# A conformer branch backward on one core: hand-made order of heads and weights, wide loads, and the place of small zero-column DMAs

## Chip, cores, metric

One core of one Trainium2 chip. The metric is the device time of one execution in microseconds, the median of the runs of a kernel. PE is the tensor engine, DVE the vector, ACT the scalar, POOL the GpSimd engine, SP the engine that issues most DMAs.

## The reference

Forward and vector-Jacobian product of one block with an attention branch and a local branch, B, T, D, K = 2, 4000, 144, 5, all bf16; the kernel returns the output and the gradients of all eight inputs.

```python
def _fwd_reference(x, w_qkv, w_att_out, w_mlp_in, dw_csgu, w_mlp_out, dw_merge, w_merge):
    xa = _layernorm(x, axis=-1)
    qkv = jnp.einsum('btd,de->bte', xa, w_qkv)
    ...
    p = _softmax(scores, axis=-1)
    attn = jnp.einsum('bts,bsd->btd', p, v)
    glob = jnp.einsum('btd,de->bte', attn, w_att_out)
    h = _gelu(jnp.einsum('btd,de->bte', xc, w_mlp_in))
    ...                       # u, g; layernorm of g; five taps of dw_csgu give gc
    loc = jnp.einsum('btd,de->bte', u * gc, w_mlp_out)
    m = jnp.concatenate([glob, loc], axis=-1)
    ...                       # five taps of dw_merge
    m = m + mc
    return x + jnp.einsum('btc,cd->btd', m, w_merge)

def reference(..., grad_out):
    _out, _vjp = jax.vjp(_f, x, w_qkv, ...)
    return (_out, *_vjp(grad_out))
```

## The kernel before

Each of the two batches runs a head (layer norm, transposes, projections of x and of the gradient, group by group), an attention, and a tail (sums and output). Batch 0's head makes the fused weights as well. The parts that matter here follow; "..." marks cuts.

The taps of the fused weights, one small product for each column of taps:

```python
            for kt in range(2):
                for kk in range(5):
                    if h == 0:
                        nc.vector.tensor_scalar(A[:, kt, 4 - kk, :], UT[h][:, kt, :], W.wm[:, h, kt, kk:kk + 1], None, op0=ALU.mult)
                    else:
                        nc.gpsimd.tensor_scalar(A[:, kt, 4 - kk, :], UT[h][:, kt, :], W.wm[:, h, kt, kk:kk + 1], 1.0, op0=ALU.mult, op1=ALU.mult)
                    nc.gpsimd.tensor_scalar(Bz[:, kt, 4 - kk, :], Wmh[:, h, kt, 128:D], W.wm[:, h, kt, kk:kk + 1], 1.0, op0=ALU.mult, op1=ALU.mult)
```

The head's loop, whose engine order a scheduler settles. The second half of the weights comes after it:

```python
        for s in range(NGR + 2):
            if s < NGR:
                stA(s)                     # gradient: transposes, goT, go80
            if 0 <= s - 1 < NGR:
                stT(s - 1)                 # normalised x: transposes, xaT and R
            if s == NGR:
                nc.sync.dma_start(S.R_d[:], R[112:128, :])
                ...                        # loads of slices of R into ra, rb: four in batch 0, eight in batch 1
            if 0 <= s - 2 < NGR:
                stB(s - 2, ...)            # pq, pb, Q_t, dug, B_t
            ...
        if wts:
            wts.second(ps_t, ps_2)
```

Memory for shifted rows. Its edges must be zero, so its construction sends two tiny DMAs. The local branch makes two of these a batch and then asks for its first rows of R, stored by the head; the tail makes two more:

```python
class Taps:
    def __init__(self, k, name):
        self.a = k.tc.dram_tile([80, self.L], BF, name=name)
        ...
            self.nc.sync.dma_start(self.a[:, 2:4], k.zero[0:80, 0:2])
            self.nc.sync.dma_start(self.a[:, self.L - 4:self.L - 2], k.zero[0:80, 0:2])

def local_steps(k, W, b, S, es, ps, Q):
    ...
    gnC = Chan(k, W, wk, ps, "gnC%d" % b)      # each holds one Taps
    dgC = Chan(k, W, wk, ps, "dgC%d" % b)
    ...
    def load_R(p):
        nc.sync.dma_start(Rz[p % 2][112:128, :], S.R_d[:, p * 256:(p + 1) * 256])
    load_R(0)
```

The tail of batch 0 ends with a store of sums. Its buffer `grs` lies in a pool that is given up with the tail; the next head's pools take over that memory:

```python
            grs = pp.tile([128, 4, D], F32, name="grs")
            for n_ in range(2):
                nc.scalar.copy(grs[:, 2 * n_:2 * n_ + 2, :], ...)
            nc.sync.dma_start(k.A.gr_d[:], grs[:])
        ...
        # phase_head of the next batch
        first = S.ab.tile([128, 16, 128], BF, tag="ST", bufs=3, name="go80f")
```

## Time and profile before

| quantity | value |
|---|---|
| time | 1294.5 us, median of 3 (1293.1 to 1294.8) |
| span of the profiled execution | 1288.0 us (that execution took 1289.9) |
| PE busy | 1211.8 us, 94% |
| granted clock | 0.993 |

The profiled execution was 3 to 5 us faster than the timed ones.

How to read what follows. A stage is a window in us from the start of the span. A wait line has who waited (engine, output tile, source line), "<-", who ended the wait, then total us, number of waits and the longest. A chain line has start, duration and what ran. A timeline line has start, duration, engine, line, operation and tiles; "SPq" is SP's issue of a DMA, and the DMA itself goes on after it. Names that come back often: gs are gradient rows as loaded, g is POOL's copy of their narrow part, and go80f holds that part transposed; pq and pb are the head's products of a group; pS and pD are the score products of attention, and X the products that follow from them; ph is the local branch's first product, which reads Rz, the rows of R loaded back; EF are the tail's sums for weight gradients; hT is ACT's copy of the tail's transposes pt, and po are its output products. The prediction shows the stage table, the waits and the chain of this kernel.

### The profile page before, as it was taken

What the parts mean: (1) busy time and instruction counts of PE and PEld (TensorE: products, weight loads), DVE (VectorE), ACT (ScalarE), POOL (GpSimd) and SP (SyncE); (2) the same over time, 40 slices, a digit from 0 to 9 for tenths busy, and PEclk for the clock granted to TensorE, in tenths of its full rate; (3) what the DMA queues carried; (4) which work ended last, traced back from release to release, by engine and by line L of the source; (5) the groups of instructions that cost most, each with busy time, mean ns of one, the idle gap of its engine ahead of it and who ended that gap; (6) DMA issues with size and microseconds to landing.
All of it is one profiled execution on the core that took longest, in us unless ns stands there. A gap on an engine that the chain in (4) does not pass through costs nothing.

```text
span 1288.0 us, 39900 instructions
## 1 busy us (share of the span) xinstructions
PE 1211.8 (94%) x15116; PEld 949.9 (74%) x15116; DVE 962.3 (75%) x3293; ACT 843.5 (65%) x2498; POOL 558.8 (43%) x1033
## 2 busy tenths in 40 slices
PE   4899999999999999998989999999999999998996
PEld 2657777777777777788975777777777777778994
DVE  4656778888888788857735677888878878885674
ACT  2667777767767766546646767777777767664542
POOL 6412444545444453257611244444544445324650
PEclk9999999999999999999999999999999999999998
DMA  6378989898989989887775889899888999987861
GB/s 185 88 142 147 156 155 159 155 167 151 161 151 159 170 155 165 151 190 216 202 220 109 152 156 152 153 169 170 148 160 153 154 170 155 164 154 182 238 168 29
DMA packets 634223, 205.51 MB, mean 160 GB/s; under 512 B 577183, under 2 KB 631556, under 8 KB 633988
## 3 DMA queue, kind: packets, MB, share of 16 engines
q1 hardware_dynamic: 627472, 197.54, 80.6%
q10 hardware_dynamic: 6548, 5.33, 1.7%
q8 instruction: 120, 1.97, 0.6%
q14 instruction: 83, 0.68, 0.2%
HBM read 46.22 MB, written 21.79 MB: 53 GB/s over the span
## 4 chain that ended last, share of the span: by engine, by line
PE 71%; DVE 13%; DMA 4%; issue 4%; ACT 4%; POOL 3%; SPq 1%; ACTq 0%; DVEq 0%; POOLq 0%
PE y L1911 15%; PE pS L1865 9%; PE X L1933 9%; PE X L1934 8%; PE pD L1865 7%; PE pS L1861 5%; DVE Sm L1875 5%; PE pc L1573 3%; PE pb L1467 2%; PE po L2088 2%; PE EF L2063 1%; DVE jg L1792 1%; PE gr L2159 1%; DVE acc L1949 1%; ACT Qs L1894 1%
## 5 line engine op out<-in xcount | busy, mean ns | idle before, releaser
L1875 DVE SCALAR_TENSOR_TENSOR Sm<-pD,Pm 128x500 bf16<-128x500 f32 x512 | 325.7, 673 | 80.3 <-PE pD L1865 47.6
L1873 ACT ACTIVATE Pm<-pS 128x500 bf16<-128x500 f32 x512 | 295.5, 586 | 41.2 <-PE pS L1865 38.3
L1933 PE MATMUL X<-Qs,Sm 128*128 128x144 bf16 x2048 | 285.6, 226 | 9.3 <-DVE acc L1949 8.9
L1946 POOL TENSOR_TENSOR acc<-xs,acc 128x432 f32<-128x432 f32 x150 | 168.5, 1123 | 280.5 <-ACT xs L1945 280.0
L1934 PE MATMUL X<-Bt,Pm 128*128 128x144 bf16 x2048 | 285.4, 226 | 0.7 <-DVE Bt L1898 0.7
L1934 PEld LDWEIGHTS <-Pm 128*128 128x128 bf16 x2048 | 199.9, 98 | 11.9 <-issue 11.3
L1933 PEld LDWEIGHTS <-Sm 128*128 128x128 bf16 x2048 | 199.8, 98 | 1.5 <-issue 0.9
L1911 PEld LDWEIGHTS <-PT 128*128 128x128 bf16 x2048 | 136.5, 97 | 30.7 <-issue 2.4
L1911 PEld LDWEIGHTS <-ST 128*128 128x128 bf16 x2048 | 136.4, 97 | 27.6
L1945 ACT COPY xs<-X 128x432 f32<-128x432 f32 x150 | 77.9, 519 | 111.4 <-PE X L1934 103.4
L1949 DVE TENSOR_TENSOR acc<-X,acc 128x432 f32<-128x432 f32 x180 | 104.0, 578 | 53.9 <-PE X L1934 53.2
L1873 ACT ACTIVATION_READ_ACCUMULATOR Pm<-pS 128x1 f32 x512 | 105.0, 205 | 0.0
L1861 PE MATMUL pD<-rb,QBr 16*128 16x500 bf16 x448 | 96.0, 378 | 3.3 <-DVE Sm L1875 2.8
L1865 PEld LDWEIGHTS <-BTm 128*128 128x128 bf16 x512 | 49.8, 98 | 59.9 <-issue 1.6
L1861 PE MATMUL pS<-rb,QBr 16*128 16x500 bf16 x448 | 91.9, 380 | 0.1
L1792 DVE SCALAR_TENSOR_TENSOR jg<-gnC,dgC 128x256 bf16<-128x256 bf16 x160 | 89.6, 560 | 1.0
L1921 POOL TENSOR_TENSOR B_t<-zd,yd 128x144 bf16<-128x144 f32 x64 | 34.0, 531 | 113.0 <-ACT zd L1920 112.7
L1865 PEld LDWEIGHTS <-QTm 128*128 128x128 bf16 x512 | 29.1, 97 | 72.5 <-issue 72.5
L1865 PE MATMUL pS<-rb,QTm 128*128 128x500 bf16 x256 | 76.9, 382 | 0.0
L1865 PE MATMUL pS<-ra,QTm 128*128 128x500 bf16 x256 | 76.5, 381 | 0.0
L1911 PE MATMUL y<-rb,PT 128*128 128x144 bf16 x1024 | 74.3, 226 | 1.0 <-ACT zd L1920 1.0
L1911 PE MATMUL y<-ra,PT 128*128 128x144 bf16 x1024 | 74.3, 226 | 1.1 <-ACT zd L1920 1.1
(626 smaller groups left out, 2895.0 us busy)
## 6 DMA issues: line engine op xcount, KB each, us to landing
gs<-in_grad_out_dram SPq DMA_DIRECT2D x24, 720.0 KB
dh_d<-dh SPq DMA_DIRECT2D x32, 144.0 KB
dhr<-dh_d SPq DMA_DIRECT2D x16, 288.0 KB
gs<-in_grad_out_dram SPq DMA_DIRECT2D x8, 540.0 KB
xg<-in_x_dram SPq DMA_DIRECT2D x21, 144.0 KB
dug_d<-dug SPq DMA_DIRECT2D x16, 144.0 KB
dug<-dug_d SPq DMA_DIRECT2D x32, 72.0 KB
ug_d<-ug SPq DMA_DIRECT2D x32, 72.0 KB
```

The source lines that it names most:

```text
L1573: nc.tensor.matmul(pc[:, q, 0:128], t[:, q * 128 + m:q * 128 + m + 128], W.dg[:, (4 - m) if back else m, :], start=(m == 0), stop=(m == 4))
L1792: nc.vector.scalar_tensor_tensor(jg[:], a_[:, m:m + 256], 1.0, d_[:, 2:258], op0=ALU.mult, op1=ALU.mult, accum_out=dws[:, p, m:m + 1])
L1861: nc.tensor.matmul(o_[h][:, 0:SC], jt[i // 4][2][rr, i % 4, :], S.XR[c2][rr, 0:SC], start=True, stop=False)
L1865: nc.tensor.matmul(o_[h][:, 0:SC], jt[i // 4][w][:, i % 4, :], S.xaT[:, c0:c0 + SC], start=False, stop=True)
L1873: nc.scalar.activation(P[:, pb, c1:c1 + SC], o_[h][:, 0:SC], ACT.Exp, accum_out=ld8[:, 0, n_:n_ + 1])
L1875: nc.vector.scalar_tensor_tensor(Sm[:, pb, c1:c1 + SC], o_[h][:, 0:SC], 1.0, P[:, pb, c1:c1 + SC], op0=ALU.mult, op1=ALU.mult, accum_out=l ...
L1911: nc.tensor.matmul(y[:, w, :], src[:, jj, :], S.xaa[:, j, :], start=(j == 0), stop=(j == NBK - 1))
L1933: nc.tensor.matmul(X[:, jj, :], Sm[:, i % NP, j * 128:(j + 1) * 128], Qs[:, i % 4, :], start=(kk == 0 and jj == 0), stop=False, skip_group ...
L1934: nc.tensor.matmul(X[:, jj, :], P[:, i % NP, j * 128:(j + 1) * 128], Bt[:, i % 4, :], start=False, stop=(kk == 1), skip_group_check=True)
L1945: nc.scalar.copy(xs[:, 0:nj, :], X[:, 0:nj, :])
L1946: nc.gpsimd.tensor_tensor(a_, xs[:, 0:nj, :], a_, op=ALU.add)
L1949: nc.vector.tensor_tensor(a_, X[:, 0:nj, :], a_, op=ALU.add)
```

## The change

The intent: less idle PE outside attention. Parts: (1) tap products as wide broadcast operations; (2) loads in order of need, with masks, pads and zeros made while they travel; (3) the head in a hand-made order instead of the scheduler's, with the second half of the weights as pieces between groups; (4) in tail 0, the gradient loads of the next batch a step earlier, its normalise a step later, the reload (`fill`) half a step later; (5) zero columns of all four Taps of a batch sent as its attention begins.

```diff
-        for s in range(NGR + 2):
-            ...
-        if wts:
-            wts.second(ps_t, ps_2)
+        with tc.manual_schedule():
+            ...                                  # heads, taps1, keys, taps, rows, groups 0 and 1
+            for n in range(-1, NGR):
+                if 1 <= n + 2 < NGR:
+                    stT(n + 2)
+                if n == 3:
+                    jit0()
+                if n >= 0:
+                    stB(n, *tiles())
+                if 1 <= n + 2 < NGR:
+                    stA(n + 2)
+                if wts and n + 3 < NGR:
+                    nrm.shift(n + 3)
+                    nrm.apply(n + 3)
+                ...                              # narrow, stats, power, take_go, dug stores
+                if n == 5:
+                    spread()                     # R_d store and the slices of R
+                if n == 4:
+                    jit()
+                if rest:
+                    next(rest, None)             # a piece of the second half of the weights
@@ taps
+            nc.vector.tensor_tensor(self.A[0][:, kt], self.UT[0][:, kt, :].unsqueeze(1).to_broadcast([128, 5, D]),
+                                    self.wr[:, 0, kt, :].unsqueeze(2).to_broadcast([128, 5, D]), op=ALU.mult)
+            ...                                  # Bz on DVE the same way, A[1] on POOL
@@ local_steps
+    zero = on.tile([128, 2], BF, name="lo_zero")
+    nc.gpsimd.memset(zero[:], 0.0)
-    gnC = Chan(k, W, wk, ps, "gnC%d" % b)
-    dgC = Chan(k, W, wk, ps, "dgC%d" % b)
+    gnC = Chan(k, W, wk, ps, "gnC%d" % b, zero)
+    dgC = Chan(k, W, wk, ps, "dgC%d" % b, zero)
+    S.taps = [Taps(k, n + "80_%d" % b, zero) for n in ("y", "u")]
     ...
     load_R(0)
@@ attention
-        local_steps(k, W, b, S, es, ps_f, Q)
         with tc.manual_schedule():
+            local_steps(k, W, b, S, es, ps_f, Q)
@@ tail
+                if hf == 0 and 0 <= g - 2 < NGR:
+                    fill(g - 2)
                 ...
-                if hf == 1 and 0 <= g - 1 < NGR:
-                    fill(g - 1)
-                    for lag, f_ in ((4, nrm.apply), (3, nrm.power), (2, nrm.stats), (1, nrm.load)):
+                    for lag, f_ in ((5, nrm.apply), (4, nrm.shift), (3, nrm.power), (2, nrm.stats), (1, nrm.load)):
-                    if NPR <= h < NPR + 3:
-                        take_go(k, nxt, 1, h - NPR, nrm.ld)
+                    if NPR + 2 <= h < NPR + 4:
+                        narrow_go(k, nxt, h - NPR - 2, nrm.ld)
+                if nrm and NPR - 1 <= h < NPR + 2:
+                    take_go(k, nxt, 1, h - NPR + 1, nrm.ld)
```

(Cut: the weights' own code, two PSUM pools with 4 and 3 buffers instead of 3 and 4, the wide x loads, one normalise in four from DVE to POOL.)

## The prediction

> **What bounds the kernel now.** I began with the busy time by stage, since the 94% mean of PE (TensorE) says nothing about where the rest is. Each row gives the window, its length, the busy time (and instructions) of PE, PE's weight loads, DVE (VectorE), ACT (ScalarE) and POOL (GpSimd), then granted clock, DMA share and GB/s.
>
> ```profile
> 0.00:64.00 64.00, 40.98 (x359) 28.89 (x359) 34.98 (x208) 30.42 (x84) 32.76 (x95) 0.99 0.49 136
> 64.00:557.00 493.00, 480.70 (x5808) 362.10 (x5808) 391.22 (x1275) 346.30 (x1049) 207.79 (x355) 0.99 0.89 157
> 557.00:650.00 93.00, 86.74 (x1374) 84.42 (x1372) 61.49 (x243) 54.79 (x143) 56.87 (x114) 1.00 0.76 210
> 650.00:680.00 30.00, 25.66 (x290) 22.06 (x287) 12.31 (x36) 16.68 (x44) 5.58 (x16) 0.94 0.66 195
> 680.00:1173.00 493.00, 480.61 (x5850) 363.42 (x5848) 392.51 (x1276) 346.14 (x1047) 207.99 (x355) 1.00 0.90 156
> 1173.00:1288.00 115.00, 97.11 (x1450) 89.04 (x1447) 69.80 (x255) 49.11 (x134) 47.79 (x100) 0.97 0.54 151
> ```
>
> The rows are head, attention, tail of batch 0, then the same of batch 1. The two attentions take 986 of 1288 us and PE is busy for 97.5% of them; the change hardly touches them, so they stay. What it can win is idle PE in the rest: 23 us in head 0, 6.3 in tail 0, 4.3 in head 1, 17.9 in the last tail (12 of them after 1245 us, in the end sums that are not changed). Some 40 us at most.
>
> Second, PE's waits in head 0 (total us, times, longest), and the chain of waits through it (start, length, what).
>
> ```profile
> PE pr L1431 <- POOL g L1428: 8.4, 3, 7.0
> PE pm L1425 <- DMA gs<-in_grad_out_dram: 5.7, 1, 5.7
> ```
>
> ```profile
> 4.26 4.98 DMA gs<-in_grad_out_dram
> ...
> 9.83 1.04 POOL rstdx L1376
> ...
> 18.06 2.41 POOL w_Bz L1224 x8
> 20.47 0.35 POOL w_A L1223
> ...
> 26.83 0.25 POOL w_Bz L1224
> 27.08 0.44 POOL g L1428
> 27.57 0.65 PE pr L1431 x4
> ...
> 63.80 0.53 PE pS L1861
> ```
>
> From 18 to 27 us POOL makes 30 tap products (20 w_Bz of a mean 293 ns, 10 w_A of 381 ns in the table of groups: 9.7 us), and the g copy that PE needs stands behind them: PE waits 7.0 us in one piece, though every input of the copy has long landed. The loop over eight groups then runs from 28 to 58 us.
>
> Third, windows where the clock or PE looked odd in the 40 slices (28 to 58 is the loop, 58 to 66 the weight work behind it, 62 to 69 the first steps of attention, 652 to 660 the start of head 1).
>
> ```profile
> 28.00:58.00 30.00, 24.75 (x249) 19.36 (x247) 20.00 (x101) 19.93 (x53) 14.01 (x31) 1.00 0.34 95
> 58.00:66.00 8.00, 7.96 (x59) 4.68 (x59) 3.61 (x24) 4.93 (x21) 0.62 (x2) 0.77 0.51 136
> 62.00:69.00 7.00, 7.00 (x37) 4.11 (x37) 1.17 (x10) 4.16 (x16) 0.62 (x2) 0.52 0.33 87
> 652.00:656.00 4.00, 0.40 (x4) 0.34 (x5) 0.11 (x1) 0.85 (x2) 2.09 (x8) 1.00 1.06 308
> 656.00:660.00 4.00, 3.64 (x35) 3.50 (x35) 1.60 (x5) 1.57 (x3) 0.46 (x1) 0.57 0.80 270
> ```
>
> In the loop all engines have room: PE 82%, DVE and ACT 67%. The weight work is 7.6 us for which no group work is left to share PE, and around it the clock drops to about half, so 62 to 69 us is PE "busy" at half the work. Head 1 shows the same pair: 3.6 us of idle PE, then 3.5 us at 0.57.
>
> Fourth, what head 1's idle waits for, in its chain, and the issue times of the SP queue and PE at the start of attention 0.
>
> ```profile
> 650.48 5.29 DMA gr_d<-grs
> 655.89 0.43 DVE go80f L1434
> ```
>
> ```profile
> 67.39 0.83 SPq L1669 DMA_DIRECT2D Rz<-R_d  x2
> 68.28 0.41 SPq L1515 DMA_DIRECT2D y<-w_zero  x1
> ```
>
> The first Rz matmul of attention starts at 69.72: 2.3 us from issue to use, with five zero-column DMAs ahead of it on that queue and three behind.
>
> **What the Trainium skill says.** "TensorE: Matmul & The Clock Gate", Part 1, HAM clock gate: an idle array runs at 1.2 GHz and gets 2.4 GHz after about 3.4 us of sustained work. The trace agrees: 0.57 for about 3.5 us after a 3.6 us gap. "GPSIMD Engine Reference", 3.1 Elementwise: a tensor_tensor costs some 2.6 cycles an element on GpSimd against 1 on the DVE. Here POOL's 128x432 product takes 1123 ns, 2.6 ns an element, so dearer than the page's 2.2; small ones are nearly all fixed cost (128x16 in 293 ns, 128x144 in 381). "Perfetto Trace Analysis", TensorE instruction: ACT, DVE and GpSimd are strict FIFO, as g behind the taps shows. "DMA: Bandwidth & Descriptors", Two DMAs through the same engine are not ordered: a load of stored data must wait for the store's completion. R_d to Rz and y to r are such pairs, so in a hand-made order the place of each store and load on its queue sets when data arrives.
>
> **The change, part by part.**
>
> Taps in head 0. 40 small products become a few wide ones with a broadcast tap: A of the first half and Bz to DVE (2 of 128x720, some 0.8 us each, estimated at one element a cycle, and a small one), A of the second half to POOL in two of 720 elements, 720 x 2.6 = 1.87 us each. 9.7 us of POOL become 3.7, in two pieces between groups. The 7.0 us stall goes.
>
> Start. Loads are issued in order of need and masks, pads and zeros are made meanwhile. Group 0's x is one DMA and issued first: landed near 2.8 us, its statistics done at 5.2, the rstd power (1.04 us a time on POOL) at 7.5, one wide tap product until 9.4, g of group 0 at 10.8, its transposes at 12.5, the weight rows at 15.4 us. There the loop starts, against 28.
>
> Loop. PE has about 3.2 us a group including a share of the weight work, so it doesn't bound. With a hand-made order each group passes around one cycle of in-order ACT: transposes stT .46, pq .25, pb 2 x .73, latency .17, dug .34, B_t .32, goT copy .6, the ACT applies .92, semaphores .05 = 4.6 us, from the durations of these groups in the trace of before. Before, the scheduler ran 3.57 us a group. So: end of pb(0) at 22.3, four cycles to 40.7, then three lighter groups and the queued weight pieces, 9.9 us: the loop ends near 50.6 us (57.8 before), and nothing of the 7.6 us weight tail follows, since it lies in the loop's gaps. Attention could begin near 51 in place of 65.3.
>
> New wait on Rz. In the new order all eight zero-column DMAs of a batch stand on SP after the last dug store and ahead of the Rz load: 8 x .43 = 3.5 us, and 2.3 to landing with issue, plus .4 for the store: Rz lands at loop end + 6.2. PE gets there at + 2.7 to 3.3 (pS and history matmuls first). So PE waits about 3 us in both batches. First Rz matmul: 50.6 + 6.2 = 56.8, against 69.7: gain 12.8 us.
>
> Head 1. The grad loads are issued a step earlier and the narrow copies of two groups move to the tail, so the 5.3 us gr_d store no longer holds up the transposes: 3.6 us of idle and 1.7 of cold clock go, 4 to 5 us in all, of which the Rz wait of 3 us takes most, and nine more DMAs on SP about 0.6. Net 0.7.
>
> Tails. The y and u reloads (fill) move from the middle of a step to the start of the next, and ACT, which issues them, no longer stands before its hT copies; in the last tail PE waits 2.7 us for hT in two waits, in tail 0 about 1.3. The g wait of tail 0 (4.2 us in 3) should shrink with the earlier loads and a later apply. I count 3 us for both tails.
>
> Sum: 12.8 + 0.7 + 3.0 = 16.5 us. 1294.5 - 16.5 = 1278.
>
> **Rivals.** (a) All of it hides: the Rz wait doesn't come because the queue drains before the loop ends (the stores of early groups are long out), the loop holds 3.3 to 3.8 us a group, and head 0 ends at 46. Then head 0 gains 19, head 1 5, tails 4: 28 us, 1266. For it: 67% busy DVE and ACT; against it: the cycle adds up to 4.6 from measured parts. (b) New waits take the gain: PE waits on R copies now on ACT, on Rz and on the late reload in the tails, where a reload moved half a step (about 2.7 us) later has only its former slack of 5.57 us DMA against the step to live on. Then head 0 gains 9, head 1 loses 2, tails 0 or -2: 1287 to 1290. For it: two stores and loads in a row per group, whose order is now fixed. (c) The clock: a loop with PE 65 to 80% busy could be granted half speed, some 3 us more; against it, the loop of before at 82% held 1.00. The cold stretch could also just move to the Rz wait, as a gap of 3 us is close to the 3.4 of the page; 1 to 2 us a batch.
>
> **Range and chances.** Head 0 is 12.8 +- 5, the other two +- 3 each: 7 in all. Range 1268 to 1288, prediction 1278. The 2% line is 1268.6, a gain of 25.9 us, out of 40 us idle: it needs (a) nearly whole, 0.13. Slower by 2% needs a loss of 26 us where only heads and tails were touched: 0.01. Within 2%: 0.86.
>
> **What would show each step.** Start: first pb matmul at 16 to 18 us, no POOL wait of PE over 2 us. Loop: pb of successive groups 4 to 5 us apart for groups 1 to 4, waits of PE on ACT. End: first pS near 51 us, no run of weight matmuls alone. Rz: a PE wait of about 3 us on the DMA of Rz, in each batch, behind eight zero-column issues on SP. Head 1: no 3.6 us gap at its start, clock 1.00 there. Tails: waits on hT under 1 us. The prediction is wrong if attention begins before 47 or after 56 us, if PE doesn't wait for Rz, or if the attention windows of 493 us change by more than 2 us, which I take as untouched.

## The result

The changed kernel took 1289.5 us (median of 4, 1288.4 to 1293.5), the kernel before 1293.9 (median of 4). The ratio is 0.997, with a 95% interval of 0.995 to 1.000. A ratio is the mean time of one kernel's fast runs over that of the other's of the same rounds, so it is not quite the ratio of the medians. The profiled span is 1286.6 us against 1288.0.

Some 16 us were forecast and about 4 came. The stage table of the changed kernel, with bounds moved to where its stages lie, shows PE as idle as before; the columns are those of the prediction's stage table.

```profile
0.00:51.00 51.00, 38.51 (x369) 28.38 (x370) 34.44 (x174) 30.19 (x83) 32.05 (x74) 1.00 0.67 187
51.00:547.00 496.00, 479.79 (x5804) 361.50 (x5803) 391.21 (x1273) 346.23 (x1045) 208.54 (x354) 1.00 0.90 154
547.00:640.00 93.00, 87.21 (x1373) 84.50 (x1371) 61.53 (x243) 54.25 (x144) 56.60 (x113) 1.00 0.76 206
640.00:670.00 30.00, 25.43 (x285) 21.79 (x283) 12.27 (x37) 16.21 (x42) 5.16 (x16) 0.89 0.63 187
670.00:1171.00 501.00, 482.83 (x5853) 364.10 (x5852) 391.57 (x1276) 347.18 (x1048) 209.48 (x356) 0.99 0.90 154
```

Row 1: the head needs 51 us up to attention where it needed 64, and PE idles 12.5 us in it instead of 23. Row 5: the second attention stage now takes 501 us for the PE work of 493.

Windows cut by hand blur a loss at a border. I therefore took, in both traces, the start of the same matmuls as marks: the first and last X product of each attention and the last EF product of each tail. Lengths of the stages between the marks, in us:

| stage | before | after | change |
|---|---|---|---|
| start to first X (head 0 and first steps of attention) | 96.90 | 85.91 | -10.99 |
| attention 0 | 465.78 | 466.33 | +0.55 |
| tail 0 | 69.87 | 70.04 | +0.17 |
| last EF to first X of batch 1 (head 1) | 77.41 | 85.76 | +8.35 |
| attention 1 | 465.73 | 465.47 | -0.26 |
| tail 1 | 69.34 | 68.20 | -1.14 |
| end sums and close | 42.97 | 44.85 | +1.88 |
| sum | 1288.01 | 1286.56 | -1.45 |

Head 0 won 11 us and head 1 gave back 8.4. PE's waits in the changed kernel, first around head 0, then around head 1:

```profile
PE ph L1804 <- DMA Rz<-R_d: 3.1, 1, 3.1
PE fw L1360 <- DVE w_c L1361: 3.0, 1, 3.0
PE tp L1478 <- POOL g L1436: 1.8, 1, 1.8
```

```profile
PE ph L1804 <- DMA Rz<-R_d: 5.8, 1, 5.8
PE tp L1473 <- DVE go80f L1481: 4.2, 1, 4.2
```

POOL's 7.0 us are gone, and there is no weight tail behind the loop: the last pb ends at 50.85 us and the first pS starts at 50.78. Two waits on Rz have come, and the wait on go80f is still there. The chain shows both in head 1, and SP's issues show why Rz is late.

```profile
641.39 5.18 DMA gr_d<-grs
646.69 0.43 DVE go80f L1481
...
677.46 1.89 DMA Rz<-R_d
679.48 0.40 PE ph L1804
679.88 0.53 PE pS L1975
680.41 0.94 PE pS L1979 x2
```

```profile
671.60 0.99 SPq L1520 DMA_DIRECT2D dug_d<-dug  x2
672.68 0.39 SPq L1625 DMA_DIRECT2D gnC_d<-lo_zero  x1
673.13 0.43 SPq L1626 DMA_DIRECT2D gnC_d<-lo_zero  x1
...
675.48 1.40 SPq L1625 DMA_DIRECT2D u<-lo_zero  x1
676.92 0.42 SPq L1626 DMA_DIRECT2D u<-lo_zero  x1
677.46 0.82 SPq L1783 DMA_DIRECT2D Rz<-R_d  x2
```

Eight DMAs of 80 x 2 elements stand on SP from 672.68 to 677.34 us, 4.7 us, between the head's last store and the load that PE waits for. The kernel before had sent the zero columns of both batches as the first attention began, so that in batch 1 its Rz load stood behind none. After the wait two pS products take 0.94 us where they take 0.53 at full clock. This window has the clock at 0.76 in the wait and 0.68 after it:

```profile
671.00:680.00 9.00, 3.17 (x25) 1.85 (x24) 0.62 (x2) 2.21 (x9) 0.00 (x0) 0.76 0.20 44
680.00:684.00 4.00, 4.00 (x25) 2.29 (x22) 1.59 (x5) 2.48 (x8) 0.00 (x0) 0.68 0.00 0
```

### The profile page after: what moved, and what is told of

It is laid out like the page before. It is cut to its first block, busy times and chain, and to the rows that moved or that the text cites. A ratio compares the mean times of both kernels' runs of the same rounds, so it can differ in the third digit from the quotient of the medians.

```text
span 1286.6 us, 39804 instructions
## 1 busy us (share of the span) xinstructions
PE 1210.9 (94%) x15118; PEld 949.2 (74%) x15118; DVE 960.4 (75%) x3257; ACT 843.3 (66%) x2494; POOL 559.4 (43%) x1011
## 4 chain that ended last, share of the span: by engine, by line
PE 66%; DVE 14%; DMA 6%; issue 5%; ACT 4%; SPq 2%; POOL 2%; ACTq 0%; DVEq 0%; POOLq 0%
PE y L2025 15%; PE pS L1979 9%; PE X L2047 8%; PE X L2048 8%; PE pD L1979 7%; PE pS L1975 5%; DVE Sm L1989 5%; PE pc L1684 2%; PE pb L1514 2%; DMA gs<-in_grad_out_dram 2%; DVE jg L1906 2%; DMA u<-r 1%; DVE acc L2063 1%; ACT Qs L2008 1%; PE pD L1975 1%
## 5 line engine op out<-in xcount | busy, mean ns | idle before, releaser
L1979 PEld LDWEIGHTS <-BTm 128*128 128x128 bf16 x512 | 49.9, 98 | 60.0 <-issue 2.0
```

The source lines that it names most:

```text
L1979: nc.tensor.matmul(o_[h][:, 0:SC], jt[i // 4][w][:, i % 4, :], S.xaT[:, c0:c0 + SC], start=False, stop=True)
```

## The experiments

Stage lengths are read from one trace for each kernel. How far they scatter with unchanged code: start to first X was 85.9, 86.7, 86.6, 88.2 and 88.7 us in five traces with the same head 0; tail 0 was 69.9 to 72.0 in seven traces with the changed kernel's tail code. Part of the first scatter goes with the clock: behind the 3.0 us wait on a weight product (shown above) the clock at 40 to 43 us was 1.00 in the first three of the five traces, and 0.50 in the two that took 88.2 and 88.7. The kernel before scatters too: its tail 0 took 69.9, 71.0 and 71.5 us in three traces with that tail's order, and its head 0 96.9 and 98.0 in two; its own trace is the shortest in both. A stage difference under 2 us in one trace is no evidence by itself.

**Rz load ahead of the zero columns** (changed kernel otherwise)

```diff
     zero = on.tile([128, 2], BF, name="lo_zero")
-    gnC = Chan(...); dgC = Chan(...); S.taps = [...]
     ...
     load_R(0)
+    gnC = Chan(...); dgC = Chan(...); S.taps = [...]
```

> The changed kernel with one edit: the first Rz load is issued ahead of the eight zero-column DMAs in both batches; all else is unchanged. Theory A (zero columns ahead of Rz on the SP queue cost a PE wait of 3.1 us in batch 0 and 5.8 us in batch 1, and the cold clock after it some 1.5 us each): the wait for Rz falls under 0.3 us in batch 0 and to about 1.2 us in batch 1, X of attention 0 starts 4 to 5 us earlier than in the changed kernel (near 81), attention 1 gains another 5 to 6, the run is 9 to 11 us faster than the changed kernel, about 1279. Rival B (attention would wait for something else at that place anyway, the K and Q slices or the transposes on the same queue): the Rz wait goes but X starts less than 1 us earlier, the run is within 2 us of the changed kernel.

Measured: 1279.8 us, ratio to before 0.987 (0.984 to 0.990). Head 1 is 78.94 us in place of 85.76. Its waits and SP's issues:

```profile
PE tp L1473 <- DVE go80f L1481: 4.3, 1, 4.3
PE ph L1804 <- DMA Rz<-R_d: 0.7, 1, 0.7
```

```profile
670.59 0.80 SPq L1520 DMA_DIRECT2D dug_d<-dug  x2
671.50 0.38 SPq L1780 DMA_DIRECT2D Rz<-R_d  x1
671.94 0.41 SPq L1625 DMA_DIRECT2D gnC_d<-lo_zero  x1
```

The Rz wait fell from 5.8 to 0.7 us in batch 1 and disappeared in batch 0. The order of one load against eight tiny stores is worth about 10 us in the times (medians 1289.5 and 1279.8, from different rounds). Theory A held, with one miss: the first X came at 84.6, not near 81. This trace's loop ended 2 us later than the changed kernel's (here too the clock was 0.51 at 40 to 43 us, behind the wait on the weight product), and the steps from 78.3 to 84.6 us ran at a clock of 0.73 where the changed kernel's had 1.00.

**grs in memory that the next head does not take over**

```diff
-            grs = pp.tile([128, 4, D], F32, name="grs")
+            grs = S.acc[:, 0:4, :]        # the accumulator, dead by then
```

(A first version with its own tile did not fit in SBUF.)

> The changed kernel with one edit: the tail's copy grs (2304 bytes a partition, the source of the gr_d store) lies in the accumulator, which is dead by then, and no longer in memory that go80f of the next head takes over. Theory A (go80f waits 4.2 us for the gr_d store because it is written over the memory that the store still reads; the store takes 5.2 us among 720 KB grad loads): the wait of DVE and PE at the start of head 1 (4.2 us) falls under 1 us, the first pb of batch 1 comes 4 to 6 us earlier with its cold clock gone; part of it may go into a longer wait for Rz, so the run gains 2 to 5 us. Rival B (the grad loads themselves are late, the gr_d store is only the last to land): go80f or the transposes wait for gs instead, the first transposes of batch 1 move by less than 1 us and the run stays within 1 us.

Measured: 1285.9 us, ratio 0.993. Head 1 is 79.13 us, 6.6 less than in the changed kernel. The waits in head 1:

```profile
PE ph L1804 <- DMA Rz<-R_d: 4.5, 1, 4.5
PE pb L1514 <- POOL Pm L1455: 1.4, 1, 1.4
```

The wait on go80f is gone, so the chain line "DMA gr_d<-grs" ahead of go80f was not about data: go80f never reads gr_d. It is written over memory that the store still reads. The first pb came 23.1 us after the last EF instead of 27.0. A smaller wait, for a POOL memset of pads, has come up behind it. On POOL that memset stands right behind a g copy, which had idled 2.76 us for a gradient load (645.01 us). So theory A held for the wait on go80f, with 3.9 us won at the first pb and 3.7 in the time, and what stands next in line is the gradient loads of rival B.

**The same edit in the kernel before**

> The kernel before with grs in the dead accumulator, nothing else. Theory A (its 3.9 us wait at the start of head 1 is the same reuse of memory, which neither kernel's order touches): the wait of PE on go80f goes, with it the half clock after it, last EF of tail 0 to first X of attention 1 falls from 77.4 to 72 or 73, the run gains 4 to 5 us. Rival B (in the kernel before the grad loads stand behind it): under 1.5 us.

Measured: 1290.8 us, ratio 0.998 (0.995 to 1.000). Its waits in head 1:

```profile
PE pb L1467 <- POOL Pm L1407: 2.5, 1, 2.5
PE pm L1425 <- DMA gs<-in_grad_out_dram: 1.0, 1, 1.0
PE pr L1431 <- DVE go80f L1434: 0.3, 1, 0.3
```

The kernel before, without the edit, had this line in their place:

```profile
PE pr L1431 <- DVE go80f L1434: 3.9, 1, 3.9
```

The 3.9 us wait fell to 0.3, yet head 1 became only 1.25 us shorter (76.16), the small size of rival B. Two waits of 2.5 and 1.0 us took most of it, and both lead to gradient loads: the second directly, the first through the memset of pads, which stands on POOL right behind a g copy that idled 3.09 us for gs (657.41 us). So rival B had the mechanism too. The reuse of memory was real in both kernels, but in the kernel before the gradient loads ended at nearly the same time. I had expected 4 to 5 us.

**Normalise back to a lag of four steps** (both the normalise and the reload then stand on even steps)

```diff
-((5, nrm.apply), (4, nrm.shift), (3, nrm.power), ...
+((4, nrm.shift), (4, nrm.apply), (3, nrm.power), ...
```

> The changed kernel with the normalise of the next batch in tail 0 put back from a lag of five steps to four, so onto even steps as in the kernel before; the reload (fill) stays at its new place, on even steps too. Theory A (the two moves of the change are one swap of the even and odd steps of ACT, each alone costs and both together give nothing in tail 0): tail 0 is 2 to 4 us longer than in the changed kernel (first EF to last EF 70.5 to 72.5 against 68.5), with PE waiting for hT as in the run that put fill back. Rival B (only the fill move matters): within 1 us of the changed kernel.

Measured: 1287.8 us, ratio 0.995. Tail 0 did not become longer (70.19 us against 70.04), so theory A of a swap fell in the form in which I put it. What moved was head 1: 81.23 us, where the four traces with the later normalise and none of the head repairs have 84.7 to 86.9. In its chain the store has shrunk:

```profile
641.04 3.71 DMA gr_d<-grs
644.87 0.43 DVE go80f L1481
```

Counted from the last EF, the store is issued at 17.9 us (as in the kernel before) and not 19.0, and takes 3.7 us and not 5.2; the wait on go80f is 1.6 us instead of 4.2. So the later normalise costs head 1 some 2.6 us at the first pb (24.3 us after the last EF against 27.0). That it does so by holding x buffers a step longer, which pushes loads back into the store, is argued and not shown. The median is only 1.7 us below the changed kernel's, from other rounds.

**Reload (fill) back to the middle of the step before**

```diff
-                if hf == 0 and 0 <= g - 2 < NGR:
-                    fill(g - 2)
+                if hf == 1 and 0 <= g - 1 < NGR:
+                    fill(g - 1)
```

> The changed kernel with the reload of y and u in the tails (fill) put back to the middle of the step before. The prediction's step (the move is worth about 3 us in both tails): the run is 2 to 3 us slower, PE's wait of the transposes for hT in the last tail comes back at 2.7 us. Rival (the move only trades the hT waits of transposes against those of the output matmuls): within 1 us, tail 0 within 0.5 us.

Measured: 1297.6 us, ratio 1.002, which is 8 us above the changed kernel's median (from other rounds), where 2 to 3 were expected. Tail 0 is 73.54 us, the longest of all traces, and it has a wait of a size that no other has:

```profile
PE pt L2153 <- ACT hT L2193: 4.2, 5, 1.2
```

So the move matters, in tail 0. The rest of the 8 us is only in part accounted for: in the trace, start to first X is 2.8 us longer (with the half clock named above), tail 1 is 1.0 us longer and head 1 1.0 us shorter. With the run before this one, three combinations of reload and normalise are known to be harmless in tail 0, 69.9 to 70.2 us in these traces and at most 72.0 in any: odd and even steps (the kernel before), even and odd (the changed one), even and even. Only odd and odd costs, 3.5 us here and at least 1.5 beyond the scatter. That it does so because both then stand on ACT's queue in the same half step is read from the code, not measured apart. The change moved the normalise onto odd steps and the reload off them. That avoided a collision which the kernel before did not have, so no gain in tail 0 was to be had from it. In the last tail, which has no normalise, this run is 69.18 us against 68.20, too little to tell; the wait of its transposes for hT came back at 2.1 us (2.7 expected).

**Gradient loads of batch 1 back to the old step**

> The changed kernel with one edit: the grad loads of the next batch in tail 0 stay where the kernel before has them, a step later. The prediction's step (earlier grad loads bring the gr_d store forward and save 4 to 5 us at the start of head 1): head 1 becomes 2 to 5 us longer. Rival (the store is issued when its sums end, whatever the grad loads did; loads a step later only lie closer to it or clear of it): last EF of tail 0 to first X of attention 1 stays within 1.5 us of 85.8.

Measured: 1289.9 us, ratio 0.997. Head 1 is 86.89 us, 1.1 more than in the changed kernel, with a go80f wait of 5.0 us. Within the rival's bounds: earlier gradient loads are not what brings the store forward.

**The weight piece reordered** (both small matmuls first, then both DVE products)

```diff
         for v in range(2):
             nc.tensor.matmul(pt[0:80, v * DR:(v + 1) * DR], ...)
+        for v in range(2):
             nc.vector.tensor_tensor(W.c80[0:80, v, :], pt[0:80, v * DR:(v + 1) * DR], ...)
```

The lines that suggested it, PE and then DVE of the changed kernel's timeline:

```profile
38.87 0.16 PE L1360 MATMUL fw<-w_cw,w_e 5*80 5x16 bf16 x1 [2.99 <-DVE w_c L1361]
```

```profile
37.87 0.87 DVE L1356 TENSOR_SCALAR w_dg<-w_ident,w_wcf 128x128 bf16<-128x128 bf16 x5
38.65 0.16 DVE L1361 TENSOR_TENSOR w_c<-fw,w_i 80x16 bf16<-80x16 f32 x1
```

> The changed kernel with one edit in the queued weight pieces: both small matmuls of the tap mask product go first and their two DVE products after them, instead of matmul, product, matmul, product. Theory A (PE stands 3.0 us behind DVE, which has five other products and the statistics of a group to do before the first of the two; the ACT normalise that the next transposes need was done 1.7 us before PE got there): the 3.0 us wait goes, the step from group 3 to 4 takes 4.3 to 4.6 us instead of 6.0 (and 7.6 in the runs where the clock fell to half after the wait), the loop ends 1.5 to 3 us earlier, the run gains 1 to 3 us. Rival B (another wait ends at the same time, the normalise or the copies): the step stays over 5.5 us, no gain.

Measured: 1289.0 us, ratio 0.996. The 3.0 us wait went, and the step from group 3 to 4 took 4.2 us instead of 6.0, as theory A said; PE's waits for the normalise rose from 1.1 to 2.3 us. The first pb came 0.8 us later in this trace (21.8 against 20.95) and the loop ended 1.0 us earlier (49.9 against 50.85), so the loop itself is 1.8 us shorter. The Rz wait of 3.1 us stayed. The median is 0.5 us below the changed kernel's, which alone can't be told from nothing: theory A was right about the wait and the step, and its gain of 1 to 3 us in the time was not seen in this run.

**The tap products alone, in the kernel before**

```diff
-                for kk in range(5):
-                    ...                       # 40 small products
+                tap = W.wm[:, h, kt, ::-1].unsqueeze(2)
+                (nc.gpsimd if h else nc.vector).tensor_tensor(A[:, kt], UT[h][:, kt, :].unsqueeze(1).to_broadcast([128, 5, D]), tap.to_broadcast([128, 5, D]), op=ALU.mult)
+                nc.vector.tensor_tensor(Bz[:, kt], Wmh[:, h, kt, 128:D].unsqueeze(1).to_broadcast([128, 5, DR]), tap.to_broadcast([128, 5, DR]), op=ALU.mult)
```

> The kernel before with one part of the change alone: the 30 small tap products of POOL and 10 of DVE become wide broadcast products (two of 128x720 on POOL, two on DVE, four of 128x80 on DVE). All else, the scheduler's order too, as before. Theory A (30 small POOL operations, 9.7 us in a row, hold up the g copy and with it PE): PE's 7.0 us wait for POOL shrinks by 5 to 7 us, first attention starts 5 to 7 us earlier, the run gains 5 to 7 us, about 1288. Rival B (the rstd power on POOL and the group loads set the pace of the loop, so it only waits later): the wait moves into the loop and attention starts less than 2 us earlier.

Measured: 1290.4 us, ratio 0.995. PE's 8.4 us of waits for POOL's g fell to 0.5. The first pb came at 27.2 us in place of 32.3, 5.0 us earlier, within theory A; the first X only 3.4 us earlier, as the scheduler's loop took 1.6 us more, and the run gained 4.4 us, so there theory A's 5 to 7 were missed. Not all wide products cost the same: between 18.3 and 21.8 us, where both engines were at such products, a 128x720 one took 2093 ns on DVE, and two took 1389 and 2050 on POOL; DVE's next, after POOL's, took 895. In the changed kernel, where POOL's come before and after DVE's, they took 889 and 891 on DVE, 1391 and 1392 on POOL. So of head 0's 11 us about 3 to 5 are the taps, and the rest is the order, the start and the weight tail.

**Both head repairs together**

> The changed kernel with both head repairs together: Rz load ahead of the zero columns, and grs in memory that the next head doesn't take over. Theory A (the two costs are separate stretches on one path): the stretch from the last EF of tail 0 to the first X of attention 1, 85.8 in the changed kernel and 79 with either repair, comes to 72 to 75; the run is 13 to 16 us faster than the changed kernel's median, 1274 to 1277. Rival B (they overlap: with the head earlier PE waits for the slices of R or for Rz on SP instead): 76 to 79, the run 9 to 11 us faster, no better than one repair.

Measured: 1276.1 us, ratio 0.986 (0.982 to 0.989). Head 1 is 74.95 us. One repair gave 6.8, the other 6.6, both 10.8: mostly separate stretches on one path, as theory A said, with some overlap. What is left at that place is PE's wait for the pads behind the gradient loads, now 2.3 us, and 0.8 us for Rz.

**All repairs, and stT behind pb**

```diff
             for n in range(-1, NGR):
-                if 1 <= n + 2 < NGR:
-                    stT(n + 2)
                 ...
                     stA(n + 2)
+                    stT(n + 2)
```

> Both head repairs, the weight piece reordered, and the transposes of xa (stT) put behind the group's matmuls on PE instead of ahead of them. Theory A of the loop (a group takes 4.2 to 4.3 us since one cycle passes stT, pq, pb, B_t, the goT copy and the normalise on in-order ACT; with stT behind pb the cycle has a step of slack and ACT's or PE's own work of 3.3 to 3.7 us a group bounds): groups 1 to 3 take 3.4 to 3.8 us, pb of group 4 comes 3 to 5 us earlier than in the changed kernel (44.9 there, first of the two), attention 0 starts 4 to 7 us earlier in all; the run is 1268 to 1274. Rival B (ACT was the bound of the loop all along, its work of some 4 us a group): groups still take 4.1 us or more and only the 1.5 to 3 us of the weight piece are gained.

Measured: 1279.0 us, ratio 0.988: slower than with the two head repairs alone. In head 0 the groups after the first took 4.4, 4.9, 3.7 and 2.9 us and the next one 6.0, with new waits of pb on ACT's copies of weight pieces. Head 1 became 80.70 us, 5.8 worse: R is complete later, and PE waits 1.8 us for slices of R. The forecast of 3.4 to 3.8 us a group failed. Whether the cycle I had named bounds the loop stays open, since this edit also moved PE's work between the weight pieces.

**Repairs without that move**, then **with the old lag as well**

> Both head repairs (Rz load ahead of the zero columns, grs in memory that the next head doesn't take) and the weight piece reordered; stT stays ahead as in the changed kernel. Theory A (the three stretches lie one behind the other, and moving stT is what spoiled the run that had all four): first X of attention 0 near 80 (81.6 with both head repairs alone), last EF of tail 0 to first X of attention 1 near 75, the run 1 to 2.5 us faster than with both repairs, about 1274. Rival B (an earlier end of the loop only turns into a wait for the slices of R or for Rz, issued by SP in a fixed order): no gain, 1276 to 1277.

> The same three repairs, and the normalise of tail 0 back at a lag of four steps. In the run with the lag alone head 1 became 4.5 us shorter, with the wait for gr_d 1.6 us in place of 4.2. Theory A (the longer lag holds the x buffers a step longer, so that loads and the grad loads behind them on SP come later and share the DMA rings with the gr_d store; with grs out of the way of go80f this no longer matters much): within 1.5 us of the kernel with the three repairs. Rival B (the late grad loads themselves hold head 1): 2 to 4 us faster than the three repairs, last EF of tail 0 to first X of attention 1 near 71 to 73.

Measured, in the same five rounds: 1273.0 us (0.984, 0.981 to 0.986) for the three repairs and 1270.5 us (0.982, 0.980 to 0.984) with the old lag. Heads 1 are 75.38 and 73.23 us. Theory A of the three repairs held: the first X came at 79.8 us, and the median is 3.1 us below that of both repairs (from other rounds). The last one beats both kernels, by 23 us and by 19 us at the medians. On top of the three repairs the old lag gave 2.5 us at the medians and 1.8 at the means, and the runs overlap (1270.8 to 1274.1 against 1270.4 to 1272.1). That lies between theory A's 1.5 and the 2 to 4 of rival B, whose 71 to 73 us head 1 did not quite reach; these runs do not settle it. If the later normalise still costs something with go80f out of the way, they don't show how.

## Why the prediction was wrong

It said 1278 (1268 to 1288) and 1289.5 came. By its own steps:

- **Head 0, 12.8 us to the first Rz matmul: the number was right, in part by luck.** 57.06 us against 56.8 predicted, a gain of 12.66. The pb products of the first step ended at 22.6 us (22.3 in the loop's sum; the sign "16 to 18 us" for their start, 20.95 measured, did not fit that sum), the loop ended at 50.85 (50.6), PE waited for Rz 3.1 us (about 3). Inside, groups 1 to 3 came 4.24 us apart rather than 4.6, and one step took 6.0 for a wait of 3.0 us on a weight product that I had not seen. The two errors cancelled. POOL's wide product took 1.39 us and not 1.87, so 1.93 ns an element where the prediction carried over 2.6 from a 128x432 product in f32.
- **What followed the Rz wait was named as a rival and not in the sum.** Of the 12.66 us, 1.67 were lost before the first X: five pb products at 59.7 us took 1.20 us together against 0.61. Rival (c) had 1 to 2 us a batch.
- **Head 1, a net gain of 0.7 us: this step failed.** It was a loss of 8.35. Counted from the last EF it splits so: first pb at 26.95 us instead of 24.55 (2.4 lost); pb to pS 21.0 instead of 23.0 (2.0 won by the new order); first pS to the first Rz matmul 9.2 instead of 2.6 (6.6 lost); from there to the first X 28.6 instead of 27.2 (1.4 lost, at low clock). Three terms failed:
  - The 4 to 5 us from an earlier gr_d store were not there: I read the chain line as a transfer late behind gradient loads, when it was a write waiting for the memory of a store, which grs elsewhere removes and earlier loads do not.
  - The later normalise made it worse: with the old lag the first pb came 2.6 us sooner.
  - The Rz wait was 5.8 us and not 3. In batch 1 the groups take about 2.6 us each, and SP still has slices of R to issue when PE is nearly through: eight slices (batch 0 has four) until 671.5, two stores, then the zeros. So SP began the zeros 1.0 us before PE ran out of work and not 2.3 as in batch 0; from their start to the Rz issue it took 4.8 us and not 3.8, as one of them held SP for 1.40; and from that issue to its use Rz took 2.0 us and not 1.6. These three make the 2.7 us between the two waits. My sum had 0.6 us for nine more DMAs on SP; the R_d store and the eight slices filled 6.3 (665.23 to 671.49).

  None of the marks by which I had said the prediction would be wrong came up (attention began at 50.8 us, PE waited for Rz, the attentions changed by 0.55 and 0.26 us), since none of them measured head 1; the sign for head 1, no gap and a clock of 1.00, did fail, with 4.2 us and 0.89.
- **Tails, 3 us: mis-sized.** Tail 0 gave nothing that can be seen within the scatter (+0.17; its wait for g, forecast to shrink, was 4.2 and is 3.9 us), tail 1 1.1: the line below, of the kernel before, is gone, but the output products' waits for hT and og rose from 1.6 to 2.6 us. The prediction counted waits on hT in tail 0 as if the reload caused them, though that tail had 0.5 us of the kind which the move can cure.

```profile
PE pt L2039 <- ACT hT L2079: 2.7, 2, 1.6
```

- **The end, taken as unchanged, became 1.9 us longer.** The last data store is issued 36.7 us after the last EF in both; the span ends 6.2 us later in the kernel before and 8.2 later in the changed one. All eleven traces of the changed kernel and its variants have 44.2 to 44.9 us after the last EF, the three of the kernel before and its variants 43.0 to 43.1. After that store has landed the records show only fetches of instructions (six in the kernel before, seven in the changed one) and the engines' closing semaphore instructions; 1.6 us of the difference is one pause of SP, 1283.8 to 1285.4 us, within which the extra fetch lies. I ran nothing on it; the cause stays open.

Terms: -11.0, +0.6, +0.2, +8.4, -0.3, -1.1 and +1.9 make -1.45 in the traces; the medians show 4.3. The kernel before's trace is of an execution 4.6 us under its median, so some stages won more than the table says; which, one trace can't tell. The range missed the median by 1.5 us.

## What to carry over

When an order is made by hand, write down for each DMA queue what stands ahead of the load that an engine waits for next: eight DMAs of a few bytes held one load back by almost 5 us, and the same eight behind it cost nothing that showed. A chain line "store, then write" may mean that memory is reused and not that data is late; look at whether the writer reads the store's result. And moving two things to each other's step is worth nothing if neither was in the other's way before.

## What the Trainium skill lacked or had wrong

- "DMA: Bandwidth & Descriptors", Anatomy of one DMA, gives a fixed cost of about 2.0 us for one DMA, as fitted on the GpSimd path. From SP the Rz loads landed 1.5 and 1.9 us after their issue, somewhat below it. What I found on no page is how long one issue holds SP's queue: in the changed kernel each tiny DMA held it for 0.38 to 0.43 us, 1.40 in one case, and the eight of batch 1 took 4.7 us. The slices of R took 0.51 to 1.09 us each, in both kernels.
- "TensorE: Matmul & The Clock Gate", Part 1, HAM oscillation, puts the gap that lowers the clock above about 3.4 us (the page's closing table of goals says about 3, which fits better). Here the 3.1 us wait for Rz in batch 0 of the changed kernel was enough: the clock was 0.50 from 58 to 61 us. It fell to 0.50 in all six traces with that wait, which is 3.0 to 3.4 us long in them. Behind the 3.0 us wait on the weight product it fell to 0.50 in three traces and stayed at 1.00 in four.
- No page I read tells that memory taken over between pools shows in a trace as a wait on a DMA that the waiting instruction does not read: 4.2 us on go80f, gone when the store's source lay elsewhere.
